# Hand-fixed instruction order, DMA transposes and reused SBUF regions in a linear-attention + SwiGLU block

## The chip, the cores and the metric

One Trainium2 chip, one core. The metric is the device time of one execution in microseconds (us). The kernel before takes 919.05 us (median of 4 runs, 916.17 to 919.5). Spans and traces are of one profiled execution each; a span is about 2 to 3 us shorter than the time.

Engines in the profile: PE is TensorE's matmuls, PEld its weight loads, DVE is VectorE, ACT ScalarE, POOL GpSimd, SP SyncE. A name with a q (ACTq, SPq) is that engine's queue when it issues a DMA. In both kernels TensorE's results go to PSUM, in tiles called banks, and ACT or DVE must copy or use a result (evacuate the bank) before the bank can be written again. LN is layer norm. Modulation is the scaling by 1 + ca and shift by sa of the reference; late modulation is the part of w_mod that is not needed for LN 1 (ga, sb, cb, gb).

## The reference

```python
S, D, F, H = 2048, 1024, 3584, 32
sa, ca, ga, sb, cb, gb = (silu(c) @ w_mod).reshape(6, D)       # w_mod is [1024, 6144]
h  = layernorm(x) * (1 + ca) + sa
q, k, v = heads(h @ wqkv)
phi = lambda t: where(t > 0, t + 1, exp(t)) + 1e-6
kv = einsum('hsd,hse->hde', phi(k), v);  z = phi(k).sum(s)      # sums over the whole sequence
o  = (phi(q) @ kv) / (phi(q) . z + 1e-6)
x  = x + ga * (o @ wo)
h  = layernorm(x) * (1 + cb) + sb
x  = x + gb * ((silu(h @ w_gate) * (h @ w_up)) @ w_down)
```

The sequence is worked on in four chunks of 512 rows. In matmuls of 128x128 weights with 512 columns, Q, K and V need 768, wo 256, gate and up 1792, down 896: 3712 in all.

## The kernel before

The Tile framework's scheduler and its pools decide the order on each engine. The parts that matter here:

```python
def transpose_chunk_to(hT_c, xn_list, scaleT, biasT, engines, col0=0):     # LN 1 and LN 2
    for cc in range(DC):
        tp = psum_ln.tile([P, STC, P], BF16, name="tp")
        for t in range(nt):
            nc.tensor.transpose(tp[:, t, :], xn_list[t][:, cc * P:(cc + 1) * P], ident[:])
        ...                                   # modulated out of PSUM by ACT or DVE

for sc in range(NSC):                         # four chunks
    ...                                       # LN, transposes
    for nb in range(2 * D // NB):             # K and V of the chunk
        ...
    for qc in (() if last else q_groups(...)):                  # Q of the same chunk
        ...
    for hg0 in range(0, HG, KVB):             # phi(K)^T V into PSUM, then added to SBUF
        ...
        nc.vector.tensor_tensor(out=kv_acc[...], in0=kv_acc[...], in1=kvp[...], op=ALU.add)
# then, for each 128 rows: nd (numerator, denominator), divide, PE transpose of o,
# o @ wo, LN 2, PE transposes; four of these before the first gate/up, the rest inside it
wme = ...                                     # 4 MB of w_mod first, then wkv 4 MB, wq 2 MB
for fb in range(0, FC, WDB):                  # w_down is loaded when gate/up 0 has ended
    nc.sync.dma_start(out=wd_sb[:, fb:fb + WDB, :], in_=wd_v[:, fb:fb + WDB, :])
```

## Time and profile before

| | before |
|---|---|
| time, median | 919.05 us |
| span of the profiled run | 915.7 us |
| PE busy | 862.9 us |
| one 128x512 matmul in a dense group (1.727 us / 8) | 0.2158 us |
| 3712 of them | 801 us |

The head of the page, kernel before:

```profile
span 915.7 us, 11358 instructions
PE 862.9 (94%) x4672; PEld 413.4 (45%) x4760; DVE 303.3 (33%) x568; ACT 212.2 (23%) x362; POOL 58.1 (6%) x109
```

The windows view gives each engine's busy time in stretches that I chose: until K and V of chunk 0 are done, until the KV sums of the last chunk, until the first down matmul, to the end. After the busy times come the clock granted to TensorE (1.00 is full), the mean busy share of the DMA engines and GB/s.

```profile
0.00:65.40 65.40, 37.91 (x291) 20.00 (x295) 34.97 (x104) 25.94 (x32) 9.63 (x22) 0.97 0.82 289
65.40:212.00 146.60, 142.99 (x1018) 73.57 (x1035) 63.73 (x121) 67.33 (x106) 1.57 (x5) 1.00 0.19 58
212.00:429.00 217.00, 205.50 (x1202) 103.54 (x1224) 102.95 (x196) 69.94 (x142) 46.88 (x82) 0.98 0.45 140
429.00:915.70 486.70, 476.54 (x2165) 216.27 (x2207) 101.68 (x147) 48.95 (x82) 0.00 (x0) 0.99 0.41 122
```

The first number after the stretch is its length, the next is PE. TensorE loses 27 us in the first stretch and 11.5 us in the third. The fourth is dense but for its head and its end (a trace can miss a few matmul records, and the end is a store). Busy is not the same as useful: transposes are in these numbers too.

TensorE's waits, longest in total first (total, times, longest), kernel before:

```profile
PE mT_ps L175 <- DMA wme<-in_w_mod_dram: 18.4, 4, 10.0
PE acc L265 <- DVE pk_c L220: 6.8, 3, 3.3
PE y_ps L534 <- DMA wd_sb<-in_B_w_down_dram: 3.5, 3, 1.6
```

And two lines of the timeline in the attention stage (start, length, engine, line, operation, then in brackets the idle time before it and who ended it):

```profile
217.21 0.63 PE L340 MATMUL nd<-KVZ,pqT 128*128 128x132 bf16 x8 [1.19 <-DVE KVZ L312]
...
222.70 1.06 PE L398 MATMUL g_ps<-wo_sb,oT_t 128*128 128x512 bf16 x2 [1.45 <-ACT oT_t L367]
```

TensorE waits there for each link of a serial chain; and two matmuls take 1.06 us in place of 0.59 (two Q matmuls at 242.64 us in the same timeline). The granted clock was 0.88 from 212 to 240 us.

### The profile page before, as it was taken

The page shows a single profiled execution, that of the slowest core. Times are in us where ns is not written, and L with a number is a line of the kernel's source. Part 1 is how long each engine was busy: PE and PEld are TensorE (multiplying, and loading weights), DVE is VectorE, ACT ScalarE, POOL GpSimd, SP SyncE. Part 2 cuts the span into 40 slices and gives each one's busy share as a digit, 9 for nine tenths or more (in the row PEclk, how much of TensorE's full clock was granted, in tenths as well). Part 3 has the DMA queues.
Part 4 walks back from the last instruction along what each step waited for, and adds up shares of the span by engine and source line. Part 5 has one row for each costly group of instructions (what it writes and reads, how often), then busy time and mean ns, then how long its engine had stood idle before and what let it go on. Part 6 is the DMA issues. An engine that isn't in the chain of part 4 may idle for free.

```text
span 915.7 us, 11358 instructions
## 1 busy us (share of the span) xinstructions
PE 862.9 (94%) x4672; PEld 413.4 (45%) x4760; DVE 303.3 (33%) x568; ACT 212.2 (23%) x362; POOL 58.1 (6%) x109
## 2 busy tenths in 40 slices
PE   1789999997999999998999999999999999999998
PEld 1335464444444544544444444444444444444443
DVE  4745255443665444441121222212212212122222
ACT  3526345342342422313011100111100111110000
POOL 2100000000422122120000000000000000000000
PEclk9999999998999999999999999999999999999999
DMA  9921060031215464459755542454531355511120
GB/s 330 393 104 47 4 227 1 1 92 35 104 66 158 122 184 142 123 151 352 227 153 158 149 127 70 143 158 142 155 110 61 101 157 152 143 48 64 69 69 24
DMA packets 153955, 117.13 MB, mean 128 GB/s; under 512 B 3888, under 2 KB 141104, under 8 KB 153904
## 3 DMA queue, kind: packets, MB, share of 16 engines
q1 hardware_dynamic: 144688, 91.24, 33.0%
q10 hardware_dynamic: 6912, 16.78, 5.8%
q0 software_dynamic: 2304, 8.39, 2.3%
q8 instruction: 37, 0.61, 0.3%
q14 instruction: 14, 0.11, 0.0%
HBM read 103.81 MB, written 12.58 MB: 127 GB/s over the span
## 4 chain that ended last, share of the span: by engine, by line
PE 68%; DMA 3%; DVE 2%; issue 1%; POOL 1%; ACT 1%; SPq 0%; POOLq 0%; DVEq 0%; ACTq 0%
PE y_ps L534 21%; PE u_ps L455 19%; PE g_ps L451 19%; PE a_ps L404 5%; DMA wd_sb<-in_B_w_down_dram 2%; PE tp L363 1%; ACT h2T_c L125 1%; PE nd L340 1%; DVE x_t L406 1%; DMA x_scratch<-x_t 1%; PE tp L121 1%; PE g_ps L398 0%; PE u_ps L226 0%; PE a_ps L398 0%; PE g_ps L226 0%
## 5 line engine op out<-in xcount | busy, mean ns | idle before, releaser
L455 PE MATMUL u_ps<-h2T_c,wu_blk 128*128 128x512 bf16 x877 | 212.1, 379 | 0.9
L451 PE MATMUL g_ps<-h2T_c,wg_blk 128*128 128x512 bf16 x880 | 212.2, 379 | 0.7
L534 PE MATMUL y_ps<-wd_sb,gu 128*128 128x512 bf16 x878 | 195.5, 381 | 4.4 <-DMA wd_sb<-in_B_w_down_dram 3.5
L464 DVE TENSOR_TENSOR gu<-u_ps,sg 128x512 bf16<-128x512 f32 x112 | 77.5, 692 | 296.0 <-PE u_ps L455 266.3
L458 ACT ACTIVATE sg<-g_ps 128x512 f32<-128x512 f32 x112 | 66.9, 598 | 428.8 <-PE g_ps L451 410.8
L534 PEld LDWEIGHTS <-gu 128*128 128x128 bf16 x896 | 88.0, 98 | 111.0 <-issue 6.5
L451 PEld LDWEIGHTS <-wg_blk 128*128 128x128 bf16 x896 | 87.4, 98 | 104.0 <-issue 0.2
L455 PEld LDWEIGHTS <-wu_blk 128*128 128x128 bf16 x896 | 87.3, 98 | 102.9
L265 PE MATMUL acc<-wkv_sb,hT_c 128*128 128x512 bf16 x373 | 88.0, 388 | 7.6 <-DVE pk_c L220 6.8
L537 DVE TENSOR_TENSOR yt<-y_ps,gb_bc 128x512 f32<-128x512 f32 x32 | 22.1, 692 | 155.2 <-PE y_ps L534 155.2
L265 PEld LDWEIGHTS <-hT_c 128*128 128x128 bf16 x384 | 37.5, 100 | 50.7 <-issue 9.9
L219 DVE TENSOR_SCALAR e<-e 128x512 f32<-128x512 f32 x56 | 23.6, 424 | 71.0 <-ACT e L218 71.0
L218 ACT ACTIVATE e<-acc 128x512 f32<-128x512 f32 x56 | 33.2, 603 | 54.4 <-PE acc L226 32.1
L404 PE MATMUL a_ps<-wo_sb,oT_t 128*128 128x512 bf16 x183 | 44.4, 379 | 1.3 <-DVE x_t L406 0.5
L226 PE MATMUL acc<-hT_c,wq_sb 128*128 128x512 bf16 x186 | 42.1, 379 | 0.3
L226 PEld LDWEIGHTS <-wq_sb 128*128 128x128 bf16 x256 | 24.4, 98 | 27.2 <-issue 0.5
L271 ACT CAST v_c<-acc 128x512 bf16<-128x512 f32 x32 | 18.7, 585 | 41.1 <-PE acc L265 39.3
L404 PEld LDWEIGHTS <-oT_t 128*128 128x128 bf16 x192 | 18.2, 97 | 22.2 <-issue 3.1
L265 PE MATMUL acc<-wkv_sb,hT_l 128*128 128x512 bf16 x124 | 28.0, 379 | 0.2
L102 DVE BATCH_NORM_STATS2 stats<-x_sb 128x6 f32<-128x512 bf16 x32 | 21.0, 670 | 9.2 <-DMA x_sb<-in_A_x_dram 9.2
L538 DVE TENSOR_TENSOR ob<-yt,x1r 128x512 bf16<-128x512 f32 x32 | 22.1, 692 | 1.1
L406 DVE TENSOR_TENSOR x_t<-a_ps,x_t 128x512 f32<-128x512 f32 x24 | 16.5, 687 | 17.7 <-PE a_ps L404 17.7
(216 smaller groups left out, 489.7 us busy)
## 6 DMA issues: line engine op xcount, KB each, us to landing
wg_blk<-in_B_w_gate_dram SPq DMA_DIRECT2D x56, 512.0 KB, 3.9
wu_blk<-in_B_w_up_dram SPq DMA_DIRECT2D x56, 512.0 KB, 5.0
wm_blk<-in_w_mod_dram SPq DMA_DIRECT2D x8, 1024.0 KB, 6.0
x_scratch<-x_t POOLq DMA_DIRECT2D x16, 512.0 KB, 3.9
x1r<-x_scratch ACTq DMA_DIRECT2D x16, 512.0 KB, 3.5
wd_sb<-in_B_w_down_dram SPq DMA_DIRECT2D x7, 1024.0 KB, 13.7
x_sb<-in_A_x_dram ACTq DMA_DIRECT2D x16, 256.0 KB, 6.2
wme<-in_w_mod_dram SPq DMA_DIRECT2D x4, 1024.0 KB, 12.4
```

The source lines that it names most:

```text
L218: nc.scalar.activation(out=e[:], in_=acc, func=ACT.Exp)
L219: nc.vector.tensor_scalar(out=e[:], in0=e[:], scalar1=1.0, scalar2=PHI_EPS, op0=ALU.min, op1=ALU.add)
L226: nc.tensor.matmul(acc[:], lhsT=wq_sb[:, cc, qc * P:(qc + 1) * P], rhs=hT_[:, cc, :], start=(cc == 0), stop=(cc == DC - 1))
L265: nc.tensor.matmul(acc[:], lhsT=hT_c[:, cc, t * P:(t + 1) * P], rhs=wkv_sb[:, cc, n0:n0 + NB], start=(cc == 0), stop=(cc == DC - 1))
L404: nc.tensor.matmul(a_ps[:], lhsT=oT_t[:, cc, :], rhs=wo_sb[:, cc, nb * NB:(nb + 1) * NB], start=(cc == 0), stop=(cc == DC - 1))
L406: nc.vector.tensor_tensor(out=x1_t[:, nb * NB:(nb + 1) * NB], in0=a_ps[:], in1=x_t[:, nb * NB:(nb + 1) * NB], op=ALU.add)
L451: nc.tensor.matmul(g_ps[:, 0:width], lhsT=wg_blk[:, cc, fj * P:(fj + 1) * P], rhs=h2T_c[:, cc, cs], start=(cc == 0), stop=(cc == DC - 1))
L455: nc.tensor.matmul(u_ps[:, 0:width], lhsT=wu_blk[:, cc, fj * P:(fj + 1) * P], rhs=h2T_c[:, cc, cs], start=(cc == 0), stop=(cc == DC - 1))
L458: nc.scalar.activation(out=sg[:, 0:width], in_=g_ps[:, 0:width], func=ACT.Silu)
L464: nc.vector.tensor_tensor(out=gu[:, cs], in0=u_ps[:, 0:width], in1=sg[:, 0:width], op=ALU.mult)
L534: nc.tensor.matmul(y_ps[:], lhsT=guT[sc][f][:, t * P:(t + 1) * P], rhs=wd_sb[:, f, nb * NB:(nb + 1) * NB], start=(f == 0), stop=(f == FC - 1))
L537: nc.vector.tensor_tensor(out=yt[:], in0=y_ps[:], in1=gb_bc[:, nb * NB:(nb + 1) * NB], op=ALU.mult)
```

## The change

Its intent: keep TensorE's 3712 matmuls and take away all that stands beside them. The core of it:

```diff
+    bank = [psum.tile([P, NB], F32, name=f"bank{i}") for i in range(8)]
+    M12 = const.tile([P, 28672], BF16, name="M12")     # wk, wv, wq; later gu and half of w_down
+    ...                                                # six regions, each reused by stage
+    ctx.enter_context(tc.manual_schedule())            # the order of the text is the order of each engine
+    def nextbank():                                    # five banks in turn for all matmul groups
+        b = bank[state["b"]]
+        state["b"] = (state["b"] + 1) % 5
+        return b

+    load_x(0); load_x(1); load_wme(0); load_x(2); load_x(3); load_wk(0, 2); load_wme(1); ...

+    def ln_b(st):                                      # LN 1, chunks 1 to 3
+        ln_nmr(st)
+        ...
+        nc.vector.tensor_scalar(out=xns[st % 6], in0=xs[st % 6], ...)
+        nc.scalar.dma_start_transpose(out=M4[:, sc_, :, t * P:(t + 1) * P], in_=xns[st % 6])
+    def modulate(sc_, cc, sT, c1T):                    # on DVE, in place, after the transpose has landed
+    def kv_mm(sc_, hg):                                # accumulates in banks 5 to 7 over all chunks
+        nc.tensor.matmul(kvb[b][:, i, :], ..., start=(sc_ == 0 and ...), stop=(sc_ == NSC - 1 and ...))

+    # order of matmul groups: K0 V0 | KV0 Q0 K1 V1 | KV1 K2 V2 | KV2 K3 V3 | KV3 Q1 Q2 Q3 | gate/up 0 | ...
+    # and what is put behind which group:
+        put_ln(sc, [("K", sc - 1, 2), ("K", sc - 1, 4), ("K", sc - 1, 6), ("V", sc - 1, 0), ...])
+        put(("V", 0, 2), lambda: load_late(0), lambda: load_late(1), lambda: load_late(2))
+    put(("V", 1, 4), lambda: late_fin(4), lambda: nc.sync.dma_start(out=wo, in_=wo_v))
+    # nd, divide, DMA transpose of o, o @ wo, LN 2, DMA transpose: spread over Q1..Q3 and gate/up 0
+        put(("GU", 1, 3 * i + 1), lambda i=i: load_wd(i))       # w_down inside gate/up 1
```

Chunk 0 keeps its 32 PE transposes. The other 352 become 44 DMA transposes of 256 KB: 12 for LN 1, 16 for o, 16 for LN 2. All 44 are issued by ACT.

## The prediction

> **What bounds it now.** TensorE. Page: PE busy 862.9 of 915.7 us (94%), DVE 33%, ACT 23%. The chain of waits is 68% PE. Eight 128x512 matmuls take 1.727 us in that chain, so 0.2158 us each; the program needs 3712: 801 us. The change keeps all of them. Only the other 114 us can shrink. The timeline places them:
>
> - Start, about 38 us: chunk 0's 128 K and V matmuls (27.6 us of work) end at 65.4 us. wme lands until 22.3 us, then TensorE waits at 34.8 and 47 us for DVE, and matmuls from 50 us come 0.43 us apart. The Trainium skill (TensorE: Matmul & The Clock Gate, Part 1) says the clock falls to half after about 3.4 us of idleness; this spacing agrees.
> - PE transposes: 384, 0.056 us apart; 352 lie after the start: 19.6 us. Eight identity-by-x matmuls: 1.7 us.
> - Work that stays: KV sums 7.2 us, numerator/denominator (nd) 7.4, late modulation 7.4, broadcasts 0.9: 23 us.
> - Gaps, about 26 us: between KV sums and first gate/up (212 to 262 us) the chain nd, reciprocal, multiply, transpose leaves TensorE little else, partly at half clock (windows: 0.93); 3.5 us waiting for wd at 431-436 us.
> - Tail: 4.4 us.
>
> From 437 us on TensorE is busy 49.7 of every 50 us: nothing to win.
>
> **What the change does.** 352 PE transposes and their evacuations become 44 DMA transposes of 256 KB issued by ACT. Modulation moves to DVE as bf16 SBUF operations (estimate 0.3 us each, 64 in all). KV stays in PSUM: 12 DVE accumulations and their waits go. Q of chunks 1 to 3 comes after all K/V, and the serial attention chain is spread over Q and the first gate/up. wd loads start earlier. First loads are ordered so that K of chunk 0 runs while wme and wk arrive.
>
> **Critical path after.** Start: x, wme and wk are 7.3 MB; before's first slices moved 330 to 390 GB/s, so about 24 us; then 22 remaining K matmuls, then V: chunk 0 done near 43 us instead of 65.4. Then 1344 x 0.2158 = 290, + 23 kept work, + 2240 x 0.2158 = 483, + tail 3.9: 843 us. I add 5 us for stalls that I can't place: 848, and 3 us since before's times exceed its span by that: 851 us.
>
> DVE is the fullest helper, in Q2 with o (estimate 22.7 us of 28). The DMA transposes' cost isn't in this trace. The Trainium skill (DMA: Bandwidth & Descriptors, Latency and other measured facts) gives 261 GB/s; estimate 1 us plus the 1.8 us a small store takes to land. The slack before each use is 3 to 20 us.
>
> **Prediction:** 851 us, 8 in 10 between 838 and 876. Faster by over 2%: 0.96; within: 0.03; slower: 0.01.
>
> **What would show it.** K and V of chunk 0 end at 40 to 46 us; no PE transposes after 30 us; PE idle under 0.5 us per 10 us between 45 us and the end; clock 1.0 after 30 us; gate/up 1 starts near 355 us rather than 425; gate/up and down durations unchanged.
>
> **What would make it wrong.** A DMA transpose that holds the ACT queue for 3 us or more: PSUM's five banks run out. Transposes that slow the weight loads. DVE falling behind in K (LN plus phi: 4.5 us per two groups, TensorE 3.45). Slower 512-byte wme rows.

A note on its sentence about the clock: the spacing of 0.43 us does go with a half clock (0.50 granted from 51 to 54 us), but the 3.4 us of idleness is not shown. TensorE had been idle for only 2.8 us, and the clock was still 1.00 in that gap; in the kernel after, it was 0.50 already in the last 1.5 us of a gap of 2.98 us (118 to 119.5 us).

## The result

| | before | after |
|---|---|---|
| time, median of 4 | 919.05 us | 882.19 us (880.06 to 883.53) |
| ratio of fast runs | | 0.9609 (0.9578 to 0.964) |
| span | 915.7 us | 878.3 us |
| end of V of chunk 0 | 65.4 us | 51.6 us (predicted near 43) |
| gate/up 1 starts | about 422 us (the prediction says 425) | 391.3 us (predicted near 355) |

Before overlaps the two stages: two of gate/up 1's 28 steps (32 matmuls, 6.9 us) ran before the first down matmul at 429.03 us, so I count its start as 6.9 us earlier, 422.1 us.

A ratio here is the mean time of one kernel's fast runs over the mean of the other's of the same rounds, so it is not quite the ratio of the medians quoted beside it.

It is faster, but 31 us slower than predicted, and outside my range. Head of the page, kernel after:

```profile
span 878.3 us, 10840 instructions
PE 843.1 (96%) x4361; PEld 399.2 (45%) x4446; DVE 331.5 (38%) x643; ACT 144.1 (16%) x270; POOL 58.9 (7%) x114
```

The windows, cut where K and V of chunk 0 are done, at the KV sums of the last chunk (both as before), where gate/up 1 starts, and at the end.

```profile
0.00:51.56 51.56, 43.32 (x301) 21.26 (x307) 29.42 (x82) 16.71 (x22) 6.30 (x26) 0.87 1.05 318
51.56:188.22 136.66, 116.54 (x802) 59.26 (x817) 68.03 (x154) 35.48 (x62) 4.76 (x8) 0.94 0.46 112
188.22:391.30 203.08, 202.02 (x1038) 96.97 (x1057) 130.65 (x257) 41.71 (x102) 47.82 (x80) 1.00 0.73 172
391.30:878.30 487.00, 481.24 (x2225) 221.70 (x2266) 103.41 (x151) 50.15 (x84) 0.00 (x0) 1.00 0.43 128
```

The third stretch, the attention stage that I had thought the most delicate, lost almost nothing: TensorE is busy 202.0 of 203.1 us at full clock. The loss is in the second, which I call **the K/V stretch** from here on. It holds 448 matmuls (Q of chunk 0, K and V of chunks 1 to 3; 96.7 us), three of four KV sums (5.4), late modulation and broadcasts (8.3): an estimate of 110.4 us of work in 136.7 us (about 1 us too high, for e10_all below did it in 109.5). So some 26.3 us are lost there, and DVE and ACT are busy for half and for a quarter of it: neither has too much to do. TensorE stood idle for 20.1 of these us. The rest is the slower clock in and after the waits: the granted clock was 0.94 over the stretch, and TensorE was busy for 116.5 us, where the run e1_sp below needs 109.1 at 1.00 for the same 802 recorded matmuls. TensorE's waits, kernel after:

```profile
PE bank L253 <- DVE M L235: 7.3, 5, 3.0
PE bank L268 <- DVE m L319: 5.2, 1, 5.2
...
PE bank L285 <- ACT M L271: 3.1, 2, 1.9
```

L253 and L268 are K and V, L285 the KV sums, L271 the copy of V, L235 the modulation, L250 the end of phi, L319 a small copy. The waits for w_mod and w_down of before are gone, new ones have come. The timeline shows how one of them arises (kernel after; L231 is the DMA transpose, L228 the normalised tile that it reads, L248 the Exp of phi):

```profile
84.64 0.55 DVE L228 TENSOR_SCALAR M<-M,rstd,nmr 128x1024 bf16<-128x1024 bf16 x1
...
85.22 1.25 ACTq L231 DMA_TRANSPOSE M<-M  x1
...
86.51 1.09 ACT L248 ACTIVATE e<-bank 128x512 f32<-128x512 f32 x2 [4.84 <-PE bank L334]
87.14 0.43 DVE L249 TENSOR_SCALAR e<-e 128x512 f32<-128x512 f32 x1 [1.36 <-ACT e L248]
...
88.35 1.89 PE L253 MATMUL bank<-M,M 128*128 128x512 bf16 x8 [1.89 <-DVE M L250]
...
91.14 0.55 DVE L228 TENSOR_SCALAR M<-M,rstd,nmr 128x1024 bf16<-128x1024 bf16 x1
91.71 1.58 ACTq L231 DMA_TRANSPOSE M<-M  x1
93.33 1.07 ACT L335 CAST ga_bc<-bank 128x512 bf16<-128x512 f32 x2 [5.74 <-issue]
94.29 0.61 ACT L248 ACTIVATE e<-bank 128x512 f32<-128x512 f32 x1
94.94 0.43 DVE L249 TENSOR_SCALAR e<-e 128x512 f32<-128x512 f32 x1 [3.26 <-ACT e L248]
...
96.22 0.59 PE L268 MATMUL bank<-M,M 128*128 128x512 bf16 x1 [5.20 <-DVE m L319]
```

Read it from the end. V's first matmul waits for a bank that DVE's copy frees; that copy stands behind phi; phi waits for ACT's Exp; the Exp stands behind the transpose in ACT's order; the transpose waited for DVE's tile (L228), and then held the queue for 1.58 us. DVE and ACT wait for each other in turn, and each is idle meanwhile. The second kind of wait:

```profile
104.78 1.43 ACTq L231 DMA_TRANSPOSE M<-M  x1
...
119.06 1.38 DVE L235 TENSOR_SCALAR M<-M,ca1T,saT 128x512 bf16<-128x512 bf16 x4 [11.74 <-DMA M<-M]
...
119.53 0.61 PE L253 MATMUL bank<-M,M 128*128 128x512 bf16 x1 [2.98 <-DVE M L235]
```

Here a transpose issued at 104.78 us landed only 14 us later, and K of chunk 2 waited for the modulation. The landing times of the 12 transposes of LN 1, kernel after (lines of the view of this one source line):

```profile
L231 ACTq DMA_TRANSPOSE M<-M x12: 1248/1266/3282, 46.8 to 150.5; - x12
...
DMA to landing us min/median/max: 3.0/5.2/14.2
```

The first line has the time that an issue holds the queue (ns; least, median, most), the last the time to landing.

### The profile page after: what moved, and what is told of

Same layout as the page of the kernel before. It is cut to its first block, busy times and chain, and to the rows that moved or that the text cites. A ratio compares the mean times of both kernels' runs of the same rounds, so it can differ in the third digit from the quotient of the medians.

```text
span 878.3 us, 10840 instructions
## 1 busy us (share of the span) xinstructions
PE 843.1 (96%) x4361; PEld 399.2 (45%) x4446; DVE 331.5 (38%) x643; ACT 144.1 (16%) x270; POOL 58.9 (7%) x114
## 3 DMA queue, kind: packets, MB, share of 16 engines
q10 hardware_dynamic: 51072, 24.12, 13.8%
HBM read 103.81 MB, written 12.58 MB: 133 GB/s over the span
## 4 chain that ended last, share of the span: by engine, by line
PE 88%; DVE 5%; DMA 3%; issue 1%; ACTq 1%; ACT 1%; SPq 0%; POOL 0%; DVEq 0%
PE bank L514 22%; PE bank L533 22%; PE bank L508 22%; PE bank L465 6%; PE bank L276 6%; PE bank L253 5%; PE bank L268 2%; DMA M<-M 2%; DVE stats L205 1%; DVE M L250 1%; ACTq L231 1%; PE bank L438 1%; DMA M<-in_A_x_dram 1%; DVE e L249 1%; PE bank L285 1%
## 5 line engine op out<-in xcount | busy, mean ns | idle before, releaser
L514 PE MATMUL bank<-M,M 128*128 128x512 bf16 x881 | 210.4, 379 | 0.8
L508 PE MATMUL bank<-M,M 128*128 128x512 bf16 x871 | 209.7, 379 | 1.3
L516 DVE TENSOR_TENSOR M<-bank,e 128x512 bf16<-128x512 f32 x112 | 77.5, 692 | 275.1 <-PE bank L514 265.7
L533 PE MATMUL bank<-M,M 128*128 128x512 bf16 (+1 forms) x687 | 146.9, 370 | 0.6
L511 ACT ACTIVATE e<-bank 128x512 f32<-128x512 f32 x112 | 66.8, 597 | 439.7 <-PE bank L508 403.1
L533 PEld LDWEIGHTS <-M 128*128 128x128 bf16 x924 | 90.4, 98 | 103.3
L514 PEld LDWEIGHTS <-M 128*128 128x128 bf16 x896 | 87.7, 98 | 105.7
L508 PEld LDWEIGHTS <-M 128*128 128x128 bf16 x896 | 87.3, 98 | 103.9
L537 DVE TENSOR_TENSOR M<-bank,gb_bc 128x512 f32<-128x512 f32 (+1 forms) x33 | 22.3, 675 | 149.2 <-PE bank L533 135.3
L253 PE MATMUL bank<-M,M 128*128 128x512 bf16 x246 | 61.6, 396 | 9.8 <-DVE M L235 7.3
L268 PE MATMUL bank<-M,M 128*128 128x512 bf16 x247 | 58.1, 389 | 8.5 <-DVE m L319 5.2
L465 PE MATMUL bank<-M,M 128*128 128x512 bf16 x254 | 57.8, 379 | 0.1
L248 ACT ACTIVATE e<-bank 128x512 f32<-128x512 f32 x64 | 37.5, 598 | 118.5 <-PE bank L253 56.2
L276 PE MATMUL bank<-M,M 128*128 128x512 bf16 x250 | 56.6, 379 | 0.3
L533 PE MATMUL bank<-M 128*128 128x512 bf16 x219 | 50.7, 379 | 0.3
L249 DVE TENSOR_SCALAR e<-e 128x512 f32<-128x512 f32 x64 | 27.9, 436 | 50.5 <-ACT e L248 50.5
L250 DVE SCALAR_TENSOR_TENSOR M<-bank,e 128x512 bf16<-128x512 f32 x64 | 44.3, 692 | 3.6
L253 PEld LDWEIGHTS <-M 128*128 128x128 bf16 x256 | 24.7, 100 | 40.8 <-DVE M L235 12.5
L268 PEld LDWEIGHTS <-M 128*128 128x128 bf16 x256 | 25.3, 100 | 39.3 <-issue 11.6
L465 PEld LDWEIGHTS <-M 128*128 128x128 bf16 x256 | 24.9, 98 | 29.8
L276 PEld LDWEIGHTS <-M 128*128 128x128 bf16 x256 | 24.6, 98 | 27.9
L467 DVE TENSOR_TENSOR M<-bank,M 128x512 f32<-128x512 f32 x32 | 22.1, 690 | 14.4 <-PE bank L465 14.3
```

Source lines behind the costliest of these rows:

```text
L248: nc.scalar.activation(out=e[:], in_=acc, func=ACT.Exp)
L249: nc.vector.tensor_scalar(out=e[:], in0=e[:], scalar1=1.0, scalar2=PHI_EPS, op0=ALU.min, op1=ALU.add)
L250: nc.vector.scalar_tensor_tensor(out=dst, in0=acc, scalar=0.0, in1=e[:], op0=ALU.max, op1=ALU.add)
L253: nc.tensor.matmul(acc[:], lhsT=M4[:, sc_, cc, t * P:(t + 1) * P], rhs=wk[:, cc, h * NB:(h + 1) * NB], start=(cc == 0), stop=(cc == DC - 1))
L268: nc.tensor.matmul(acc[:], lhsT=M4[:, sc_, cc, t * P:(t + 1) * P], rhs=wv[:, cc, h * NB:(h + 1) * NB], start=(cc == 0), stop=(cc == DC - 1))
L276: nc.tensor.matmul(acc[:], lhsT=wq[:, cc, qc * P:(qc + 1) * P], rhs=M4[:, sc_, cc, :], start=(cc == 0), stop=(cc == DC - 1))
```

## The experiments

Theory A: ACT's fixed order. A transpose that ACT must issue waits for DVE and then holds the queue, and the evacuation of PSUM stands behind it. Theory B: the transposes land late because weight loads are ahead of them in the DMA queues. Theory C: DVE has too much work in K (this was a risk named in the prediction). For the start: theory S1, the LN chain of the fourth x tile; S2, the loads.

The result of all, with the K/V stretch in each profile from the first KV sum of chunk 0 to the first of chunk 3:

| run | time | ratio to before | K/V stretch |
|---|---|---|---|
| after | 882.19 | 0.9609 | 136.7 |
| e1_sp | 858.57 | 0.9366 (0.9347 to 0.9386) | 112.8 |
| e2_later | 867.91 | 0.9482 (0.9456 to 0.9508) | 123.8 |
| e3_plain | 872.24 | 0.9519 (0.9502 to 0.9535) | 128.8 |
| e4_loads | 882.13 | 0.9611 (0.9581 to 0.9642) | 137.5 |
| e6_wo_ahead | 858.01 | 0.9357 (0.9336 to 0.9378) | 114.4 |
| e7_pe_ln (wrong result) | 866.89 | 0.9453 (0.9432 to 0.9473) | 118.8 |
| e7b_pe_ln | 865.71 | 0.9427 (0.9405 to 0.9449) | 121.0 |
| e8_pe_o | 877.30 | 0.9574 (0.9549 to 0.9598) | 112.8 |
| e9_sp_xfirst | 853.44 | 0.9309 (0.9289 to 0.9328) | 112.8 |
| e11_held | 858.65 | 0.935 (0.9324 to 0.9375) | 113.9 |
| e10_all | 847.90 | 0.923 (0.9211 to 0.9249) | 109.5 |

Each ratio is to the kernel before in the same rounds on the same chip. The kernel before took 916.9 to 919.1 us in the different rounds, so times of different rounds compare to within about 2 us.

### e1_sp: the transposes of LN 1 issued by SP

```diff
-        nc.scalar.dma_start_transpose(out=M4[:, sc_, :, t * P:(t + 1) * P], in_=xns[st % 6])
+        nc.sync.dma_start_transpose(out=M4[:, sc_, :, t * P:(t + 1) * P], in_=xns[st % 6])
```

> The 12 DMA transposes of the first LN are issued by SP instead of ACT; nothing else moves. Measure: the K/V stretch, from the end of chunk 0's V matmuls (51.6 us after the span's start in the changed kernel) to the first KV sum of chunk 3 (188.2 us): 136.6 us, of which about 110 us is TensorE's own work. Theory A (ACT's fixed order: an Exp or a V copy stands behind a transpose that waits for DVE and then holds the queue 1.25 to 3.3 us): ACT evacuates on time, the waits at 54-58, 86-96 and 144-150 us go, the stretch falls by 10 to 15 us and the time to about 868 us. Theory B (the transposes land late because weight loads share the DMA queues, and DVE stands in front of the modulation): these waits stay or move, the waits at 117 and 155 us stay, time within 4 us of 882. Theory C (DVE has too much work in K): no change.

Measured: 858.57 us; one word in one line brings 24 us, and the K/V stretch falls from 136.7 to 112.8 us, 2.4 us above its work. It is more than A promised, since a part of B went with it. TensorE's waits, e1_sp:

```profile
PE bank L341 <- ACT M L223: 5.0, 3, 2.6
PE bank L268 <- DVE m L319: 1.9, 1, 1.9
PE bank L253 <- DVE M L235: 1.6, 1, 1.6
```

The place of 84.64 to 86.51 us above, in e1_sp:

```profile
81.27 0.55 DVE L228 TENSOR_SCALAR M<-M,rstd,nmr 128x1024 bf16<-128x1024 bf16 x1
...
81.85 1.24 SPq L231 DMA_TRANSPOSE M<-M  x1
81.96 0.60 ACT L248 ACTIVATE e<-bank 128x512 f32<-128x512 f32 x1 [1.93 <-PE bank L253]
```

The Exp no longer follows the transpose's issue: it runs beside it, when TensorE has filled its bank. Theory C falls, as DVE's work in the stretch did not change (68.0 us busy in after, 67.7 in e1_sp, line below). The Trainium skill (Trainium Kernel Development and Optimization, Key Constraints) says that issuing DMAs from several engines only saves the sequencer's issue time. This run shows what such issue time, and the wait in front of it, can cost when ACT's queue also carries the evacuation of PSUM; the next runs show how much of the 24 us it is. The window of the K/V stretch, e1_sp:

```profile
51.65:164.40 112.75, 109.06 (x802) 56.61 (x817) 67.74 (x154) 35.20 (x60) 4.76 (x8) 1.00 0.55 139
```

Other transposes, those of o and LN 2, are still issued by ACT in this run. The 12 on SP were issued by 131.6 us and took at most 8.6 us to land; ACT issued its first at 178.00 us. No run here had transposes of two queues in flight together.

### e2_later: the transposes stay on ACT, one step later

```diff
-            lambda: (ln_a(s0 + 2), ln_b(s0 + 1)),
+            lambda: (ln_t(s0), ln_a(s0 + 2), ln_b(s0 + 1)),      # ln_t is the transpose alone
```

(and so for the other steps; the modulation moves one group later)

> The transposes stay on ACT but each stands one step (one or two matmul groups) later in the order, and the modulation one group later, so that DVE has finished the normalised tile when ACT reaches the transpose. Theory A, waiting half (ACT stands waiting for DVE): the ping-pong at 81-96 and 136-150 us goes, stretch shorter by 8 to 12 us, time about 871 us; if the holding of the queue is what costs, then only 2 to 4 us. Theory B: no gain, rather 1 to 3 us lost since the transposes land still later. Theory C: no change.

Measured: 867.91 us, stretch 123.8. The ping-pong is gone: 13 of the 24 us came from the transposes' place in ACT's order. That is ACT standing still for DVE and also some holding, as two issues near 50 us got shorter as well (2.65 and 1.97 us for 3.20 and 3.28). Two waits stayed, before K of chunk 2 and of chunk 3; of TensorE's waits only this line is clearly above e1_sp's (8.5 us for 1.6):

```profile
PE bank L255 <- DVE M L237: 8.5, 5, 4.9
```

Lines of the timeline of e2_later (L237 is the modulation, L233 the transpose):

```profile
95.49 0.65 SPq L610 DMA_DIRECT2D M<-in_A_wo_dram  x1
96.24 3.87 SPq L137 DMA_DIRECT2D M<-in_A_x_dram  x4
...
98.52 7.38 ACTq L233 DMA_TRANSPOSE M<-M  x1
...
113.00 2.67 DVE L237 TENSOR_SCALAR M<-M,ca1T,saT 128x512 bf16<-128x512 bf16 x8 [13.46 <-DMA M<-M]
```

SP has nothing left to wait for, runs ahead of TensorE and queues 3 MB of wo and x just before the last transpose. Its issue then takes 7.38 us in place of 1.25.

### e3_plain: plain copies in place of the transposes (wrong result)

```diff
-        nc.scalar.dma_start_transpose(out=M4[:, sc_, :, t * P:(t + 1) * P], in_=xns[st % 6])
+        nc.scalar.dma_start(out=M4[:, sc_, :, t * P:(t + 1) * P],
+                            in_=xns[st % 6].rearrange("p (c s) -> p c s", c=DC))
```

> Wrong result on purpose: in place of the 12 DMA transposes of the first LN, plain DMA copies of the same tile at the same place in ACT's order (h is not transposed). Theory A, waiting half: ACT still waits for DVE, so the waits at 81-96 and 136-150 us stay; time 876 to 882 us. Theory A, holding half: an issue takes about 0.35 us instead of 1.25 to 3.3, gain 6 to 10 us. Theory B in the form that the transpose itself is slow: the copies land in 3 us and the DVE waits at 117 and 155 us (16.7 us of DVE idle) go, gain 5 to 7 us; in the form that the weight loads before it delay anything: no gain there.

Measured: 872.24 us, stretch 128.8, so 8 us less in the stretch. An issue of a plain copy held ACT for 0.60 us (median), of a transpose for 1.27. The waits of A stayed, but shorter (4.2 us in place of 5.2 at the largest), and the copies landed as late as the transposes had, after up to 13.2 us. So holding the queue is a real part of A, and late landing is not a property of the transpose: it is the queue that it stands in. The check passed this result as correct, although h is not transposed for chunks 1 to 3. So the check does not see an error in these 12 transposes, and "correct" in e1_sp, e2_later, e11_held and e10_all does not vouch for them.

### e4_loads: late loads put later in SP's order

```diff
-    put(("V", 0, 2), lambda: load_late(0), ...)
+    put(("Q", 0, 0), lambda: load_late(0), ...)
-    put(("V", 1, 4), lambda: late_fin(4), lambda: nc.sync.dma_start(out=wo, in_=wo_v))
+    put(("V", 1, 4), lambda: late_fin(4))
+    put(("K", 2, 1), lambda: nc.sync.dma_start(out=wo, in_=wo_v))
```

> The first three late w_mod loads (3 MB) are issued after Q group 0 of chunk 0 instead of after V group 2, and wo (2 MB) in K of chunk 2 instead of V of chunk 1; transposes as in the changed kernel. Theory B: the issues of 3.2 us at 49 and 52 us shrink to 1.25 us, the wait for KV at 54-58 us goes, and the DVE wait of 11.7 us at 107-119 us shrinks to below 3 us; gain 5 to 8 us, time about 875 us; the waits at 86-96 and 144-150 us stay. Theory A: ACT still waits for DVE, gain under 3 us. Theory C: no change.

Measured: 882.13 us, no gain. This does not speak against B, for the edit did not do what I meant: SP issues as soon as it can, so wo went out at 110.06 us, right behind the four x tiles, whatever group stood before it in the text. DVE still waited 10.4 us. Of the transposes at 47 to 54 us three now held ACT for 1.25 to 1.47 us, but the fourth for 4.20, as the moved loads had begun at 50.42. A place in the text holds a DMA back only on a queue that itself waits for the work around it. e11_held is this test made properly.

### e6_wo_ahead: SP issues the transposes, 2 MB put ahead of them

```diff
 # on e1_sp
+    put(("K", 1, 5), lambda: nc.sync.dma_start(out=wo, in_=wo_v))     # moved here from ("V", 1, 4)
```

> The SP-issued transposes (as in the run e1_sp), but the 2 MB load of wo is placed ahead of the second transpose of chunk 2 on SP's queue instead of after the fourth. ACT is as free as in e1_sp. If a transpose that is queued behind weight loads lands late and this alone stalls DVE and TensorE (theory B as a second cause beside A), the last transposes of chunk 2 land about 5 us later, DVE waits some 5 us longer than e1_sp's 5.0 us for them, and TensorE waits 1 to 5 us before K of chunk 2; time 860 to 863 us. If only ACT's order mattered (A alone), 858 to 859 us as e1_sp.

Measured: 858.01 us, as e1_sp. DVE waited 6.3 us for the last transposes instead of 5.0, and TensorE's own waits did not grow. Loads ahead of a transpose did no harm here, where ACT wasn't held and the landing stayed inside the slack; my size for B (5 us more) was wrong.

### e11_held: e2_later, with the loads that overtook held back

```diff
 # on e2_later: wo, x tiles 12 to 15 and the first three gate/up blocks
-    nc.sync.dma_start(...)
+    nc.scalar.dma_start(...)          # at the same place in the text, so behind the transposes
```

> On e2_later (transposes on ACT, one step later; 867.9 us): wo, the last four x tiles and the first three gate/up blocks are issued by ACT at their places in the order, so that they can't be queued before the transposes of chunks 2 and 3. In e2_later SP ran ahead and queued them first; TensorE then waited 4.9 us before K of chunk 2 and 1.8 us before K of chunk 3 for a modulation that waited for a transpose. If loads that overtake the transposes are this second cause (theory B beside A), these two waits go with the half-clock matmuls after them and the time is 859 to 862 us; if the transposes on ACT's queue land late for another reason, 866 to 869.

Measured: 858.65 us, as expected, with the stretch at 113.9 us. Timeline of e11_held at the place shown for e2_later:

```profile
97.97 1.55 ACTq L233 DMA_TRANSPOSE M<-M  x1
...
100.44 0.42 ACTq L610 DMA_DIRECT2D M<-in_A_wo_dram  x1
```

The 12 transposes landed within 8.3 us at most, in place of 14.4 in e2_later, and TensorE waited 1.6 us for the modulation in place of 8.5.

So the loss of 24 us in the K/V stretch is taken away by two cures in turn: 13 us by letting ACT reach the transpose when its input is ready (after to e2_later), 10 us by keeping the loads behind it (e2_later to e11_held). e1_sp does both at once, since on SP's queue the transposes stand before those loads.

### e7_pe_ln and e7b_pe_ln: PE transposes for LN 1 again

```diff
 # on e2_later
-        nc.scalar.dma_start_transpose(out=M4[...], in_=xns[st % 6])
+        tp = nextbank()[:].bitcast(BF16).rearrange("p (c s) -> p c s", c=DC)
+        for cc in range(DC):
+            nc.tensor.transpose(tp[:, cc, :], xns[st % 6][:, cc * P:(cc + 1) * P], ident[:])
+        nc.scalar.copy(out=M4[...], in_=tp)
 # e7b_pe_ln only
-    put(("K", 1, 6), lambda: late_bc(2, ga_bc))
+    put(("K", 1, 7), lambda: late_bc(2, ga_bc))
```

> Undo a part: the 12 DMA transposes of the first LN become PE transposes (96, at the places of the run e2_later) with an ACT copy out of PSUM. Cost by the trace of before: 96 x 0.056 = 5.4 us of TensorE. No DMA wait is left in front of the modulation. If ACT's standing at the transposes and their late landing are the whole loss (A and B), the K/V stretch is 112.8 (e1_sp) + 5.4 + about 1 = 119 us against the changed kernel's 136.7, time about 865 us: the DMA transposes of this stage would then have cost the changed kernel some 18 us net. If the loss lies elsewhere (C, or PSUM banks), 882 us or more.

> e7_pe_ln was wrong because my PE transposes took turns in the five PSUM banks between the two halves of one late modulation sum, so that its bank was reused before the second half; here the ga broadcast comes one group later, which leaves that bank alone. Correct result expected, and the time of e7_pe_ln, 866 to 868 us: 5.4 us of PE transposes and some 4 us of TensorE waiting for DVE in front of them, above e1_sp's 858.6.

Measured: e7_pe_ln had a wrong result (relative error 0.26): with one more user of the five banks, the bank of a half-finished late sum came round again. e7b_pe_ln is correct at 865.71 us. Undoing the DMA transposes of LN 1 makes the kernel 16 us faster than the changed kernel; compared with e1_sp it costs 7 us. So DMA transposes were right for LN 1, and their place in ACT's queue turned a gain of 7 us into a loss of 16.

### e8_pe_o: PE transposes for o and LN 2 again

```diff
 # on e1_sp, in nd_tr and o_tr
-        nc.scalar.dma_start_transpose(...)
+        tp = nextbank()...; 8 x nc.tensor.transpose(...); nc.scalar.copy(...)
```

> The SP-issued first-LN transposes as in e1_sp, but the 32 DMA transposes of o and of the second LN become PE transposes (256) with ACT copies out of PSUM. The prediction credited 256 x 0.056 = 14.3 us to their removal from TensorE. If that is right the time is 858.6 + 14 = 873 us, up to 878 if TensorE also waits for POOL or DVE in front of a transpose; if the DMA transposes of this stage were slowing anything (weight loads of the first gate/up), less than 14 us is lost.

Measured: 877.30 us, 18.7 us more than e1_sp. 14.2 us are the 256 transposes at 0.0556 us, 4.5 us are waits, nearly all of this line, e8_pe_o:

```profile
PE bank L489 <- POOL M L481: 3.9, 4, 1.2
```

The sum that the prediction credited to these transposes is confirmed, and a little more: a DMA transpose also takes TensorE out of the chain. These 32 transposes are issued by ACT too. There ACT's order has the transpose far enough behind its input, and the third window shows no loss.

### e9_sp_xfirst: x before w_mod

```diff
 # on e1_sp
     load_x(0); load_x(1)
+    load_x(2); load_x(3)
     load_wme(0)
-    load_x(2); load_x(3)
```

> On e1_sp: x tiles 2 and 3 (0.5 MB) are loaded before the first w_mod part (1 MB). Theory S1 (the start hangs on the LN chain of the fourth x tile, whose statistics wait for x until 11.6 us in the changed kernel, and then TensorE works through K without waiting for loads): first K matmul at 15 to 16 us instead of 19.4, V of chunk 0 ends at 47 to 48.5 us instead of 51.65, time about 855 us. Theory S2 (the loads bound the start, as the prediction had it): w_mod and wk land no earlier, V ends at 51 to 52 us, time 858 to 860 us.

The start of the kernel after, in its timeline (L205 are the statistics of the third x tile, L253 the first K matmuls):

```profile
9.89 1.29 DVE L205 BATCH_NORM_STATS2 stats<-M 128x6 f32<-128x512 bf16 x2 [2.32 <-DMA M<-in_A_x_dram]
...
19.43 0.61 PE L253 MATMUL bank<-M,M 128*128 128x512 bf16 x1 [1.58 <-DVE M L235]
...
20.25 2.90 PE L253 MATMUL bank<-M,M 128*128 128x512 bf16 x8 [0.22 <-issue]
```

Measured: 853.44 us. The first K matmul comes at 16.96 us (expected 15 to 16) and V ends at 49.14 (expected 47 to 48.5): S1 in direction, with 2.5 us in place of 4. From the first K matmul on TensorE is not waiting for loads: 19.43 + 128 x 0.2158 + three times 0.81 us of modulation matmuls (from start to start) + 2.1 us of slower matmuls, 1.4 of it in the first ten (granted clock 0.60 from 19.43 to 23 us) = 51.6 us, and V ended at 51.6.

### e10_all: a version that beats both

```diff
 # on e9_sp_xfirst
-            nc.vector.tensor_copy(out=m1[:, q, :], in_=mps[:, 0:DC])
+            nc.scalar.copy(out=m1[:, q, :], in_=mps[:, 0:DC])
-    put(("K", 1, 6), lambda: late_bc(2, ga_bc))
+    put(("K", 1, 7), lambda: late_bc(2, ga_bc))
-    warm(14) ... warm(2) ... warm(2) ...
+    warm(18) ... warm(4) ... warm(4) ... warm(6, 4)     # the last six in bank 4, before K
```

> A version meant to beat both: e9_sp_xfirst (853.4 us), with the two remaining waits of the K/V stretch taken out (the late modulation's sum is copied by ACT instead of DVE, where it stood behind phi: 1.85 us; the ga broadcast one group later: 0.55 us), and with more idle matmuls on zeros in the gaps of the start, so that the first eight K matmuls run at 0.216 instead of 0.36 us. Expected: 2.4 us from the waits, 1 to 2 us from the start: 849 to 851 us. If the zero matmuls delay the transposes of the start, no more than 2.4 us.

Measured: 847.90 us (847.66 to 847.96), correct, and 1 to 3 us better than expected. The first three windows of e10_all: the start (up to e9's end of V, 2.3 us after e10_all's own; its busy time includes the idle matmuls on zeros, which do no work for the result), K/V, and attention with gate/up 0:

```profile
0.00:49.14 49.14, 45.08 (x343) 22.11 (x344) 30.04 (x83) 18.36 (x25) 6.30 (x26) 1.00 1.06 320
49.14:160.00 110.86, 110.86 (x836) 57.62 (x834) 66.77 (x149) 36.49 (x65) 4.76 (x8) 1.00 0.56 144
160.00:380.00 220.00, 220.00 (x1115) 103.80 (x1113) 134.61 (x264) 44.22 (x106) 47.81 (x80) 1.00 0.73 182
```

TensorE has no idle time at all from 49 to 380 us, and the clock is 1.00 in the start too (0.87 in the changed kernel). The first K matmuls of e10_all:

```profile
16.08 2.33 PE L253 MATMUL bank<-M,M 128*128 128x512 bf16 x10 [0.29 <-DVE M L235]
```

Ten in 2.33 us, against eight in 2.90 us in the changed kernel. The Trainium skill (TensorE: Matmul & The Clock Gate, Part 1) says that the clock rises only after some 3.4 us of sustained work; the idle matmuls give it that work. This run agrees: the first K matmuls had the full clock, where the changed kernel was granted 0.60.

## Why the prediction was wrong, and where it was right

The prediction was 848 us for the span; it was 878.3. The 30 us are two terms of its sum.

1. **"I add 5 us for stalls that I can't place" was the step that failed.** The stalls were 26.3 us in the K/V stretch (136.7 us measured, 110.4 us of work). I had costed the DMA transposes by how long they take to land and had found "slack before each use is 3 to 20 us". What hurt was where they are issued: in ACT's fixed order, ahead of the evacuation of PSUM, in front of an input that DVE had not made (13 us together, e2_later). The slack was wrong too: the transposes of LN 1 landed up to 14.2 us after issue, since loads had been queued ahead of them (10 us, e11_held), where the prediction's estimate of landing was 2.8 us. My list of dangers had "holds the ACT queue for 3 us or more", and some issues did (3.28 us), but it lacked the wait in front of the issue, and I gave it too little weight. The "DVE falling behind in K" of that list did not happen: DVE was busy for half of the stretch.

2. **The start: "about 24 us; then 22 remaining K matmuls ... near 43 us" was wrong by 8.6 us.** I took the start to be bound by loads with K hidden beside them. In fact K could begin only at 19.43 us, because the LN chain waited (2.32 us) for the third x tile, which stood with the fourth behind 1 MB of w_mod, and from there TensorE had 128 matmuls and three rounds of modulation matmuls in a row, the first at the low clock. e9_sp_xfirst gains 2.5 us from the order of loads, e10_all another 2.3 from the rest of the start (V ends at 46.82).

8.6 us and 26.3 less the 5 allowed give 29.9 of the 30.3 us; as the 26.3 rests on an estimate, the fit to 0.4 us is partly luck.

What was right: no matmul was saved and none needed to be; removing PE transposes was worth what it was costed (14.2 us for 256 of them in e8_pe_o, plus waits); the spread attention stage lost nothing (202.0 of 203.1 us busy); the wait for w_down went; gate/up and down took 487.0 us, of which 483.4 are matmuls by count. The changed kernel's own gain of 37 us is about 14 us in the start, 17 in K/V, attention and gate/up 0 together, and 6.6 after that. The last is mostly the wait for w_down with the slow matmuls around it: from 429.03 to 445.20 us before ran 48 matmuls, 5.8 us more than they need. In the middle the change took away about 21 us of PE transposes and identity matmuls and some 22 us of gaps (an estimate: what is left of before's 357 us), and gave back 26 us by its own new waits.

Open: how much of the 13 us is ACT waiting and how much is the issue itself can't be added up exactly. Nor is it shown how far the waits alone, without the fall of the clock, would have cost less. e3_plain, which halves the issue but leaves the wait, gained 8 us in the stretch, so the two seem to overlap. I did not try to take the LN chain of the start apart further.

## What to carry to other kernels

When an order is fixed by hand, ask for each DMA issue: what does it wait for, how long does it hold its queue, and what stands behind it there. Issue it from an engine whose queue carries nothing urgent, or so late that its input is surely ready; and know that a queue without waits runs ahead and puts its loads in front of yours. To cost a removed instruction is the easy half of a prediction; the waits that its replacement brings must be looked for in the order of every engine that it touches.

## What the Trainium skill lacked or had wrong

- DMA: Bandwidth & Descriptors has no figure of trn2 for how long a DMA transpose of this size holds the queue that issues it (a column for earlier generations in its trn3 table is for other sizes). Here one of 128x1024 bf16 held it for at least 1.25 us on ACT and 1.23 us on SP, against 0.60 us for a plain copy with the same pattern; with loads queued, up to 3.28 us (after) and 7.38 us (e2_later).
- The same page, Latency and other measured facts, gives 261 GB/s for a DMA transpose. By the share of the DMA engines' time it seemed dearer here. The lines of ACT's DMA queue (packets, MB, share of 16 engines over the span), before and then after:

```profile
q10 hardware_dynamic: 6912, 16.78, 5.8%
```

```profile
q10 hardware_dynamic: 51072, 24.12, 13.8%
```

  Before, 48 plain loads made it; after, 32 plain loads (12.58 MB) and 44 transposes (11.53 MB). With the plain part scaled by bytes and span (4.5%), 9.3% of 878.3 us is left, an estimate of 1.9 us of all 16 engines for each 256 KB, about 140 GB/s. This is no measured bandwidth: packet times overlap, for the same share reads 1.05 of all 16 engines in the first window of after. (51072 - 32 x 144) / 44 gives 1056 packets for each, so about 248 bytes a packet.
- The same page's rule that a transpose next to ordinary DMAs needs nothing is about correctness; the time to landing went from 3.0 us at the least to 14.2 us behind loads (after), and to 13.2 us for plain copies (e3_plain).
- Trainium Kernel Development and Optimization, Key Constraints, counts only issue time as the gain of another queue. It lacks that the issue, and its wait, also delay all other work of that engine: about 13 of the 24 us between after and e1_sp in the K/V stretch (e2_later).
